# A transform and two MLPs on one core: the buffers' addresses in SBUF moved by 64 and by 192 bytes

## The chip, the cores and the metric

One of the eight cores of one Trainium2 chip runs the program. The metric is the device time of one execution in microseconds (us); three executions were timed, and their median counts.

## The reference

```
X = fft(fft(x, axis=1), axis=2).real          # x: (2, 3008, 256), float32
x = X.reshape(6016, 256)
h = x @ w_in;   x = relu(h)**2 @ w_out         # 256 -> 2048 -> 256
h = x @ w2_in;  x = (h * sigmoid(1.702*h)) @ w2_out   # 256 -> 2048 -> 256
```

## The kernel before

The token axis is split in blocks of 512, 512 and 482 columns for each of the two sequences; features lie on the 128 partitions. A value in float32 is carried as a high part and a low part (type fp32r), and each product is three matmuls: high by high, low by high, high by low.

**Head** (about the first 38 us). The first input `xt` is loaded, folded by VectorE (`fold`, tiles `t` and `xt`) and transformed on TensorE (lines 554, 565, 638, 673). The results become `eo` tiles, the even and odd parts in high and low.

**First MLP.** 96 steps, one for each block of tokens and group of 128 hidden features. A step is six matmuls (`front1`, lines 768 to 770: moving operand `eo`, result `psa`), three VectorE instructions that put `p` and `h` together (lines 1047, 1049, 1050), relu and square on ScalarE (1058, 1059), the high part `gh` on ScalarE (1064), the low part `gl` on GpSimd or VectorE (helper `sub`, line 181), and twelve matmuls (`back`, line 783: moving operands `gh` and `gl`, result `psb`). Six more pairs of matmuls (line 745, `o02N` to `o13N`) take pieces of an `eo` block, that begin at any column, against the constant `sel_t`. Loading and splitting of all weights, and the transform of the later inputs, is interleaved. The order of all of it is written out by hand as a list of names (`ORDER`), run under a manual schedule.

**Second MLP.** 48 units of two hidden groups each. A unit has 21 matmuls (`products`, line 1103: moving operands `ya`, `yb`, `yc`, result `psc`) and 24 matmuls (`back2`, line 1119: moving operands `gh` and `gl`). Between them ScalarE and VectorE form `a1`, `u` and `g` (lines 1150 to 1155, 1186 to 1189), the high part `gh` (1164) and the low part `gl` (181). The order is that of the loop.

**Where the tiles lie.** Each partition of SBUF is filled from two sides. On the left, upward: small constants, the weights (`w`, from address 1408 on; `ya` and `yb` later reuse two of these places), the raw inputs (`raw`), the input tiles, and in the second MLP the pool `m2` with `yc`, `a1`, `u`, `g` and every second `gh`. On the right, downward from the top: a tile `edge` that nothing reads or writes, and under it `mg` (`gh`, `gl`; the pool `m3` takes its place in the second MLP), `m` (`p`, `h`), `ep` (`eo`), `np` (`n`), `zp` (`misc`, `zc`, `zs`) and `cp` (`cst`). Before the change the weights, the right side's large tiles and `m2` begin at addresses that are all the same modulo 512: 1408 for the weights, 151424 for the lowest `eo`, 200576 for a `gh` and 140672 for `yc` each leave 384.

The lines that set the places are these; `edge` and `shift` are read and written by nothing. In the last one (line 768) the weights come from the left side and the moving operand from the right.

```python
small.tile([P, 16], F32, name="shift")
...
edge = tc.alloc_tile_pool(name="edge", bufs=1, side="right")
edge.tile([P, 24], F32, name="edge")
mg = tc.alloc_tile_pool(name="mg", bufs=2, side="right", reuse_waits="tile")
...
T.matmul(o, lhsT=w[:, 0, fs], rhs=t[:, par, 0, 0:wd], start=True, stop=False)
```

Of the kernel before, what the change touches and what calls it, by code (L numbers as in the profile page):

```python
# [9 lines left out]
F32 = mybir.dt.float32  # L10
# [6 lines left out]
P = 128  # L17
# [151 lines left out]
def spectral_two_mlps_kernel(  # L169
# [49 lines left out]
    wq = ctx.enter_context(tc.tile_pool(name="wq", bufs=4))  # L219
    cv = ctx.enter_context(tc.tile_pool(name="cv", bufs=1))  # L220
    edge = tc.alloc_tile_pool(name="edge", bufs=1, side="right")
    edge.tile([P, 24], F32, name="edge")
    mg = tc.alloc_tile_pool(name="mg", bufs=2, side="right", reuse_waits="tile")
    m = tc.alloc_tile_pool(name="m", bufs=2, side="right", reuse_waits="tile")
    ep = tc.alloc_tile_pool(name="ep", bufs=3, side="right", reuse_waits="tile")
# [862 lines left out]

    m2 = tc.alloc_tile_pool(name="m2", bufs=1, side="left", reuse_waits="tile")
    m3 = None  # L1090
    yC[0] = m2.tile([P, 2, 3, NP2], F32R, tag="yc", name="yc")
    units = 8 * BLKS
    run(stage_c(0))
# [256 lines left out]
```

## Time and profile before

| | |
|---|---|
| time, median of 3 executions | 944.34 us (944.24 to 944.53) |
| the profiled execution's own time | 944.28 us |
| its span, first to last instruction | 942.5 us |
| PE busy | 934.3 us, 99% |
| DVE, ACT, POOL busy | 697.9, 566.8 and 267.8 us |
| mean granted TensorE clock | 0.999 of full speed |

The span is what the trace covers; the time is 1.78 us longer than it. The busy time of PE is that of matmuls that overlap, so it says that PE hardly ever sat idle, and not that it ran at its peak. The engines are called PE (TensorE), PEld (its weight loads), DVE (VectorE), ACT (ScalarE), POOL (GpSimd) and SP (SyncE, which issues the DMAs).

### The profile page before, as it was taken

The page shows a single profiled execution, that of the slowest core. Times are in us where ns is not written, and L with a number is a line of the kernel's source. Part 1 is how long each engine was busy: PE and PEld are TensorE (multiplying, and loading weights), DVE is VectorE, ACT ScalarE, POOL GpSimd, SP SyncE. Part 2 cuts the span into 40 slices and gives each one's busy share as a digit, 9 for nine tenths or more (in the row PEclk, how much of TensorE's full clock was granted, in tenths as well). Part 3 has the DMA queues.
Part 4 walks back from the last instruction along what each step waited for, and adds up shares of the span by engine and source line. Part 5 has one row for each costly group of instructions (what it writes and reads, how often), then busy time and mean ns, then how long its engine had stood idle before and what let it go on. Part 6 is the DMA issues. An engine that isn't in the chain of part 4 may idle for free.

```text
span 942.5 us, 10895 instructions
## 1 busy us (share of the span) xinstructions
PE 934.3 (99%) x4272; PEld 778.5 (83%) x4272; DVE 697.9 (74%) x810; ACT 566.8 (60%) x605; POOL 267.8 (28%) x144
## 2 busy tenths in 40 slices
PE   9999999999999999999999999999999999999998
PEld 9688888887877888888888888888888888888886
DVE  7999998988878788887897665665575476476453
ACT  5798997563746767686856544544454455455343
POOL 0665776542453547163123200020020011000000
PEclk9999999999999999999999999999999999999999
DMA  8421434600010041100320100110010011001001
GB/s 312 157 90 45 159 134 140 224 1 1 31 37 1 1 137 43 54 37 0 132 90 1 54 33 1 45 46 1 1 65 22 1 43 46 0 1 45 1 1 42
DMA packets 13058, 53.52 MB, mean 57 GB/s; under 512 B 1360, under 2 KB 4688, under 8 KB 9808
## 3 DMA queue, kind: packets, MB, share of 16 engines
q1 hardware_dynamic: 13008, 52.84, 15.5%
q8 instruction: 33, 0.54, 0.2%
q14 instruction: 17, 0.14, 0.0%
HBM read 37.36 MB, written 15.48 MB: 56 GB/s over the span
## 4 chain that ended last, share of the span: by engine, by line
PE 97%; DVE 2%; DMA 1%; ACT 0%; issue 0%; SPq 0%; DVEq 0%
PE psb L1119 27%; PE psb L783 27%; PE psc L1103 24%; PE psa L768 5%; PE psa L769 5%; PE psa L770 5%; PE psa L638 1%; PE psa L565 1%; PE psa L673 1%; PE psb L638 1%; DMA xt<-in_x 1%; PE psb L565 0%; DVE eo L181 0%; DVE h L1050 0%; DVE t L486 0%; DVE t L490 0%
## 5 line engine op out<-in xcount | busy, mean ns | idle before, releaser
L783 PE MATMUL psb<-gh,w 128*128 128x512 f32 (+1 forms) x768 | 216.0, 387 | 0.0
L181 POOL TENSOR_TENSOR gl<-h,gh 128x1024 fp32r<-128x1024 f32 (+1 forms) x62 | 155.7, 2514 | 136.9 <-PE psb L783 74.6
L783 PEld LDWEIGHTS psb<-gh,w 128*128 128x128 f32 x768 | 144.0, 188 | 28.3 <-issue 0.4
L1119 PE MATMUL psb<-gh,w 128*128 128x512 f32 (+1 forms) x576 | 164.3, 387 | 0.0
L1187 DVE TENSOR_TENSOR g<-u,psc 128x1024 f32<-128x1024 f32 (+1 forms) x48 | 57.6, 1201 | 116.5 <-PE psc L1103 116.5
L1064 ACT CAST gh<-h 128x1024 fp32r<-128x1024 f32 (+1 forms) x96 | 98.4, 1034 | 50.1 <-PE psb L783 34.8
L1189 ACT ACTIVATE g<-g 128x1536 f32<-128x1536 f32 (+1 forms) x48 | 70.4, 1467 | 95.7 <-DVE g L1187 95.7
L1119 PEld LDWEIGHTS psb<-gh,w 128*128 128x128 f32 x576 | 108.3, 188 | 21.1
L783 PE MATMUL psb<-gl,w 128*128 128x512 f32 (+1 forms) x384 | 117.4, 387 | 0.0
L181 DVE TENSOR_TENSOR gl<-g,gh 128x2048 fp32r<-128x2048 f32 (+2 forms) x50 | 110.7, 2217 | 0.4 <-ACT gh L1164 0.4
L1058 ACT ACTIVATE h<-h 128x1024 f32<-128x1024 f32 (+1 forms) x76 | 79.2, 1042 | 23.8 <-DVE h L1050 23.8
L888 POOL TENSOR_TENSOR ue<-raw 128x512 f32<-128x512 f32 (+1 forms) x11 | 19.9, 1832 | 250.9 <-DMA raw<-ydram 244.5
L1164 ACT CAST gh<-g 128x2048 fp32r<-128x2048 f32 (+2 forms) x50 | 90.5, 1814 | 0.1
L1119 PE MATMUL psb<-gl,w 128*128 128x512 f32 (+1 forms) x288 | 88.2, 387 | 0.0
L783 PEld LDWEIGHTS psb<-gl,w 128*128 128x128 f32 x384 | 72.3, 188 | 13.9
L1047 DVE SCALAR_TENSOR_TENSOR p<-n,w1n_t,psa 128x512 f32<-128x512 f32 (+1 forms) x96 | 70.2, 731 | 18.1 <-PE psa L770 17.8
L1059 ACT ACTIVATE h<-h 128x1024 f32<-128x1024 f32 (+1 forms) x76 | 79.7, 1049 | 2.4
L1049 DVE TENSOR_TENSOR h<-p,psa 128x512 f32<-128x512 f32 (+1 forms) x96 | 65.1, 678 | 17.6 <-POOL gl L181 4.3
L768 PE MATMUL psa<-eo,w 128*128 128x512 f32 (+1 forms) x192 | 75.3, 392 | 0.5 <-DVE zc L594 0.3
L769 PE MATMUL psa<-eo,w 128*128 128x512 f32 (+1 forms) x192 | 74.4, 388 | 0.6 <-DVE eo L181 0.6
L1186 ACT ACTIVATE g<-psc 128x512 f32<-128x512 f32 (+1 forms) x48 | 28.4, 592 | 76.6 <-PE psc L1103 76.6
L770 PE MATMUL psa<-eo,w 128*128 128x512 f32 (+1 forms) x192 | 74.4, 387 | 0.0
(178 smaller groups left out, 1530.9 us busy)
## 6 DMA issues: line engine op xcount, KB each, us to landing
ydram<-o SPq DMA_DIRECT2D x14, 512.0 KB, 3.4
xt<-in_x SPq DMA_DIRECT2D x5, 1024.0 KB, 7.1
cst<-in_dfts SPq DMA_DIRECT2D x8, 576.0 KB, 5.7
raw<-in_w1i SPq DMA_DIRECT2D x4, 1024.0 KB, 5.1
raw<-in_w1o SPq DMA_DIRECT2D x4, 1024.0 KB, 6.4
raw<-in_w2o SPq DMA_DIRECT2D x4, 1024.0 KB, 5.7
raw<-in_w2i SPq DMA_DIRECT2D x4, 1024.0 KB, 6.6
raw<-ydram SPq DMA_DIRECT2D x4, 1024.0 KB, 4.8
```

The costliest lines, as they stand in the source:

```text
L181: eng.tensor_tensor(out=o, in0=a, in1=f32(b), op=ALU.subtract)
L768: T.matmul(o, lhsT=w[:, 0, fs], rhs=t[:, par, 0, 0:wd], start=True, stop=False)
L769: T.matmul(o, lhsT=w[:, 0, fs], rhs=t[:, par, 1, 0:wd], start=False, stop=False)
L770: T.matmul(o, lhsT=w[:, 1, fs], rhs=t[:, par, 0, 0:wd], start=False, stop=True)
L783: T.matmul(acc[j][ec][:, s, 0:wd], lhsT=w[:, hl, e0:e0 + P], rhs=(gh, gl)[gi][:, s, 0:wd], start=(first and hl == 0 and gi == 0), stop=(la ...
L1058: A.activation(out=hv, in_=hv, func=AF.Relu)
L1059: A.activation(out=hv, in_=hv, func=AF.Square)
L1064: A.copy(st["gh"][:, :, 0:wd], st["h"][:, :, 0:wd])
L1103: T.matmul(bank, lhsT=w[:, hl, slot * P:(slot + 1) * P], rhs=x[:, yl, 0:wd], start=(first and hl == 0 and yl == 0), stop=(hl == 1), skip_g ...
L1119: T.matmul(o[:, s, 0:wd], lhsT=weights[1, 1, f // 4][:, hl, e0:e0 + P], rhs=g[:, 2 * i + s, 0:wd], start=(f == 0 and hl == 0 and g is gh), ...
L1164: A.copy(gh[:, at], gs[u - 1][:, at])
L1189: A.activation(out=g[:, 1:4], in_=g[:, 1:4], func=AF.Gelu_apprx_sigmoid)
```

## The change

The unused tile `edge` shrinks from 96 to 32 bytes in each partition, so that everything on the right side lies 64 bytes higher. A new unused tile `shift2` of 192 bytes stands ahead of the second MLP's left pool, so that `yc`, `a1`, `u`, `g` and the `gh` in that pool lie 192 bytes higher. The weights, the raw inputs, the input tiles `xt` and `t`, `ya` and `yb` stay where they were.

```diff
     edge = tc.alloc_tile_pool(name="edge", bufs=1, side="right")
-    edge.tile([P, 24], F32, name="edge")
+    edge.tile([P, 8], F32, name="edge")
     mg = tc.alloc_tile_pool(name="mg", bufs=2, side="right", reuse_waits="tile")
...
     m2 = tc.alloc_tile_pool(name="m2", bufs=1, side="left", reuse_waits="tile")
     m3 = None
+    m2.tile([P, 48], F32, name="shift2")
     yC[0] = m2.tile([P, 2, 3, NP2], F32R, tag="yc", name="yc")
```

In the built programs each engine has the same instructions in the same order, with the same waits on the same semaphores at the same counts; line numbers behind the second edit and buffer numbers alone differ. The addresses are:

| tiles | address before (bytes in the partition) | after | modulo 256 before, after |
|---|---|---|---|
| weights `w`, `ya`, `yb`, `raw`, `xt`, `t`, `ue` | 1408 and on | the same | 128, 128 |
| `cst`, `misc`, `n`, `eo`, `p`, `h`, `gh`, `gl`, `o` on the right | 116096 and on | 64 more | 128, 192 |
| `zc` | 132864 | 64 more | 0, 64 |
| `yc`, `a1`, `u`, `g`, `gh` in `m2` | 140672 and on | 192 more | 128, 64 |
| PSUM and DRAM tiles | | the same | |

## Rows read from the trace of the kernel before

**Rows 1.** The page: busy time of each engine; granted clock in 40 slices.

```profile
PE 934.3 (99%) x4272; PEld 778.5 (83%) x4272; DVE 697.9 (74%) x810; ACT 566.8 (60%) x605; POOL 267.8 (28%) x144
PEclk9999999999999999999999999999999999999999
```

**Rows 2.** Windows: stretch, its us, busy us of each engine, granted clock, DMA.

```profile
0.00:38.00 38.00, 35.83 (x241) 30.82 (x242) 32.26 (x55) 21.35 (x48) 10.23 (x13) 1.00 0.77 291
38.00:240.00 202.00, 200.66 (x929) 166.07 (x928) 186.13 (x248) 153.54 (x160) 113.72 (x51) 1.00 0.26 93
240.00:445.00 205.00, 205.00 (x913) 169.19 (x912) 166.31 (x207) 141.12 (x150) 100.05 (x52) 1.00 0.11 39
445.00:607.00 162.00, 162.00 (x716) 134.06 (x715) 119.03 (x119) 93.21 (x95) 22.66 (x16) 1.00 0.13 45
607.00:942.50 335.50, 330.86 (x1481) 278.36 (x1479) 194.13 (x185) 157.53 (x153) 21.09 (x12) 1.00 0.07 25
38.00:138.00 100.00, 99.74 (x440) 81.03 (x439) 94.99 (x127) 90.92 (x93) 68.05 (x28) 1.00 0.29 101
```

**Rows 3.** Waits of PE's matmuls over the span: us, times, longest.

```profile
PE psa L444 <- DVE still L267: 1.1, 1, 1.1
PE psa L638 <- DVE h L1050: 0.8, 1, 0.8
PE psa L769 <- DVE eo L181: 0.6, 1, 0.6
```

**Rows 4.** The chain that ended last, in order of time: start us, us, what.

```profile
32.70 2.52 DVE eo L181
...
35.26 0.50 PE psa L769
...
444.68 2.73 PE psc L1103 x12
...
541.37 2.72 PE psb L1119 x12
...
549.53 2.04 PE psc L1103 x9
...
642.60 2.64 PE psb L1119 x12
```

**Rows 5.** Groups of equal form: count, then busy us, mean ns, idle before.

```profile
L1049 DVE TENSOR_TENSOR h<-p,psa 128x512 f32<-128x512 f32 x64 | 44.0, 688 | 12.9 <-POOL gl L181 3.9 <-DVE p L1047 1.5 <-DMA ydram<-o 1.0
L1153 DVE TENSOR_TENSOR u<-a,psc 128x512 f32<-128x512 f32 x32 | 22.0, 686 | 29.1 <-ACT a L1150 29.1
L1064 ACT CAST gh<-h 128x1024 fp32r<-128x1024 f32 x64 | 66.7, 1050 | 23.3 <-PE psb L783 17.1 <-DVE h L1056 4.3 <-issue 1.1
L368 ACT CAST w<-ue 128x1024 fp32r<-128x1024 f32 x10 | 10.5, 1047 | 0.0
L181 POOL TENSOR_TENSOR gl<-h,gh 128x1024 fp32r<-128x1024 f32 x42 | 108.9, 2597 | 75.5 <-PE psb L783 30.6 <-ACT gh L1064 26.5 <-DVE h L1050 5.8
L181 POOL TENSOR_TENSOR w<-ue,w 128x1024 fp32r<-128x1024 f32 x8 | 23.7, 2958 | 17.0 <-ACT w L368 16.9
```

**Rows 6.** Timeline of TensorE around `o13N` (line 745): start us, us.

```profile
366.92 0.51 PE L745 MATMUL psa<-eo,sel_t 128*128 128x376 f32 x2
367.27 0.40 PE L768 MATMUL psa<-eo,w 128*128 128x512 f32 x1
```

**Rows 7.** Timeline of VectorE and GpSimd at the end of the head.

```profile
29.93 0.94 DVE L181 TENSOR_TENSOR eo<-ht,eo 128x756 fp32r<-128x756 f32 x1
32.61 2.59 DVE L181 TENSOR_TENSOR eo<-ht,eo 128x268 fp32r<-128x268 f32 x1
31.60 3.31 POOL L181 TENSOR_TENSOR w<-ue,w 128x1024 fp32r<-128x1024 f32 x1 [1.77 <-ACT w L368]
```

**Rows 8.** DMA issues by tile (times, KB each, us to landing), and the wait on one.

```profile
ydram<-o SPq DMA_DIRECT2D x14, 512.0 KB, 3.4
DVE h L1049 <- DMA ydram<-o: 1.2, 3, 0.6
```

## The prediction

> **What bounds the kernel now.** I first read the page's busy rows: PE is busy in 99% of the span, DVE in 74%, ACT in 60%, and the granted clock is at its upper level, 2.4 GHz, in all 40 slices [rows 1]. Busy time of overlapping matmuls doesn't show their pace, so next come the windows [rows 2]. From 240 to 607 us PE is busy in every microsecond; from 38 to 240 us it misses 1.3 us, in the first 38 us 2.2, and behind 607 us 4.6, nearly all of it the last copies and the last store. PE's own waits are 1.1, 0.8 and 0.6 us at the longest [rows 3]. So what bounds the kernel is the pace of the matmuls, and no other engine's work, outside a head of some 35 us.
>
> The pace is in the chain by time [rows 4]: twelve matmuls of 512 columns in 2.72 us, 226.7 ns each (nine with `yc` in 2.04, the same), and twelve of 482 columns in 2.64 us, 220.0 each. At 2.4 GHz 512 columns are 213.3 ns and 482 are 200.8, so a matmul of 512 pays 13.3 ns beside its columns and one of 482 pays 19.2. How many there are follows from the code: 96 steps of 18 and 48 units of 45 are 3,888, two thirds of them (2,592) with 512 columns. 2,592 x 226.7 ns + 1,296 x 220.0 ns = 587.6 + 285.1 = 872.7 us of the 942.5. The rest is the head (36 us), the transforms between the steps, the stalls above and the tail.
>
> **The change, part by part.** It adds and removes no instruction. The order on each engine, the waits, their counts, the transfers and their sizes stay. The two edits have one answer, so they are costed together: their cost is the change of each instruction's duration when its operands begin elsewhere. The two tiles themselves cost nothing, since nothing writes them. What the rows say for each engine:
>
> - *DVE and ACT.* The same work on tiles of the right side and of the left takes the same time. A sum of 128x512 takes 688 ns with its tiles on the right and 686 on the left; a cast of 128x1024 takes 1,050 on the right and 1,047 on the left [rows 5]. These tiles begin at the same place modulo 512, so the rows prove only that the side doesn't matter. I take 0 for the change. The ends: below, -2 us (the head's blocked instruction, under the rivals); above, +4.5 us (a rival too). The cover is DVE's idle time, 15.9 us from 38 to 240 us; without it the slower work would show in PE's stalls one for one.
> - *PE.* The moving operands on the right (`eo`, `gh`, `gl`) and in `m2` (`yc`, half of `gh`) move against the weights. Twelve of a unit's products have `ya` and `yb`, which stay: 48 x 12 = 576, and so 3,312 matmuls change their distance from their weights. Before, all these distances are 0 modulo 512, and a trace with one value of the cause can't show its effect. One place differs: line 745, where `eo` is read from column 106 of a block on, 424 bytes into it, against weights that begin at 576. There two matmuls of 376 columns take 0.35 us [rows 6], 175 ns each; 376 columns are 156.7 ns, so each pays 18.3 ns. That is between the 13.3 and the 19.2 of the aligned ones. The nearest row thus says that distance costs nothing, and I take 0. The ends are the only spread in that overhead that the trace shows, 19.2 - 13.3 = 5.9 ns to either side: 3,312 x 5.9 ns = 19.5 us less or more.
> - *POOL.* Its low parts on the right take 2,597 ns in the mean and those of the weights, as large, on the left 2,958 [rows 5]; the 3.31 us of one that lies over a DVE instruction [rows 7] shows what spreads them. I take 0; the ends are those of DVE, since POOL itself idles half of the first MLP.
> - *DMA.* Stores and loads of tiles on the right begin 192 instead of 128 bytes past a multiple of 256. A 512 KB store takes 3.4 us from issue to landing, and in the first MLP waits on it come to 1.2 us in 3 times, of DVE, not of PE [rows 8]. I take 0; even a tenth more on each, 0.34 us, would only lengthen DVE's three waits by 1 us, before the 15.9 us that it has idle.
>
> A rule that speaks against the change is in the Trainium skill, DMA: Bandwidth & Descriptors, section How a descriptor splits into AXI transactions: a piece that doesn't start at a multiple of 256 bytes begins with a transaction from the boundary below, and pays for the bytes ahead. If that holds for the SBUF side, a row of 4,096 bytes goes from 132 beats of 32 bytes to 134, 1.5%, or by an estimate from that page 0.05 us of the store's 3.4; the sum would stay where the rows have it. No run here shows it yet.
>
> The sum: 944.28 us for the profiled execution (942.5 of span and 1.78 around it), plus 0. It lies 0.06 us under the median of 944.34, so the forecast is **944.3 us**. The three times lie within 0.3 us of each other, and 0.2% of the time, 1.9 us, is about what a measurement of this kernel can tell from no change.
>
> **The rivals.**
>
> 1. *PE's reads depend on the distance to the weights, and the new distance is better.* For it: each matmul pays 13.3 or 19.2 ns that its columns don't explain, so there is something to win, and with PE never idle each nanosecond counts 3,312 times, 3.3 us. Against it: rows 6. From 0.57 ns a matmul on it is faster by 1.9 us; at 2.4 ns it gives 8 us, 936.3; at the end, 924.8.
> 2. *The same dependence, and the new distance is worse*: slower, on the other side from no change. For it: the tiles leave the multiples of 128 bytes on which weights and moving operands stood together. Against it: rows 6 again, where the operand begins 40 bytes past a multiple of 256. It decides from 0.57 ns a matmul; at 2.4 ns it gives 952.3, at the end 963.8. In both cases the products with `ya` and `yb` would keep their 226.7 ns.
> 3. *Side engines get slower* because a tile that begins off a 128-byte line costs more per row. From 38 to 138 us DVE is busy for 95.0 of 100 us and PE for 99.7 [rows 2], so this is where it would show. 5.0 us of idle time cover a growth of 5%; PE falls behind by 1.9 us at (5.0 + 1.9) / 95.0 = 7%, about 50 ns on a 690 ns sum. At 10% the loss is 9.5 - 5.0 = 4.5 us: 948.8. Against it: no pair of DVE or ACT in rows 5 differs by more than 3 ns, though none lies off a 128-byte line.
> 4. *The head falls another way.* Ahead of the first hidden step DVE makes `eo` from 128x268 elements in 2.59 us, while 128x756 took 0.94 just before; POOL's 3.31 us instruction lies over the slow one, and PE waits for the result until 35.26 us [rows 4, 7]. A few tens of nanoseconds elsewhere could put DVE ahead of POOL. The gain is at least 2.59 - 0.94 = 1.65 us, 942.6, at most nearly the 2.59: 942.0 is a fair value, just past what can be told.
>
> The Trainium skill, SBUF: State Buffer, section Who interferes with whom, has the rule for the last: VectorE with two SBUF inputs and GpSimd reading SBUF lock each other out for a whole instruction, and nothing else contends. The blocked 2.59 us agree; by that page PE waits for nobody and rivals 1 to 3 would have no cause, but it doesn't speak of addresses, so it doesn't exclude them.
>
> **How the numbers follow.** No change to within 1.9 us: 0.55, which holds the small forms of all four. Rival 1 past 0.57 ns: 0.16. Rival 4, far enough to be told: 0.08. Rival 2: 0.12. Rival 3: 0.09. So faster 0.24, same 0.55, slower 0.21. For the range I go into the PE rivals to 2.4 ns, and no further: 8 us to either side, 936 to 952. That takes in rivals 3 and 4 whole, 0.17, and about half of rivals 1 and 2, 0.14, and with the 0.55 it makes 0.86; since the ends of the unknown are guesses of mine I don't narrow it.
>
> **What would show it.** Right: twelve matmuls of lines 783 and 1119 still take 2.72 and 2.64 us in the chain; the sum at line 1049 stays at 688 ns and the cast at line 1064 at 1,050; PE's busy time in the window from 240 to 607 us is full, and the windows' borders in the program (first product of line 1103 at 444.7 us [rows 4]) haven't moved by more than 1 us. Wrong: a pace other than 226.7 ns on lines 768 to 783 and 1119, and on `yc`, with `ya` and `yb` unchanged (rivals 1, 2); DVE's or ACT's means up by 5% and PE with new waits on `gl` or `psa` before 138 us (rival 3); `eo` of 268 elements under 1 us and the first hidden step ahead of 35 us (rival 4). The prediction is wrong if PE's pace hangs on where its operands lie, which the trace of before couldn't test.

## The result, and the profile after

The changed kernel takes 950.11 us (949.93 to 950.31, 4 executions) against 944.29 us (944.17 to 944.53, 4) of the kernel before on the same chip: a ratio of 1.0061, 95% interval 1.0044 to 1.0079. It is 5.8 us slower. The range of 936 to 952 us holds the time; the forecast of no change was wrong, and it went the way of rival 2.

The page and the windows of the changed kernel, to compare with [rows 1, 2] (stretch, its us, busy us of PE, PEld, DVE, ACT, POOL, granted clock, DMA):

```profile
PE 941.5 (99%) x4272; PEld 779.6 (82%) x4272; DVE 696.4 (73%) x810; ACT 565.9 (60%) x605; POOL 267.1 (28%) x144
38.00:240.00 202.00, 201.79 (x928) 166.16 (x928) 184.56 (x248) 153.28 (x160) 114.87 (x51) 1.00 0.27 93
240.00:445.00 205.00, 205.00 (x907) 168.37 (x906) 166.09 (x206) 139.72 (x149) 100.23 (x52) 1.00 0.11 39
```

PE is busy for 7.2 us more, at the same granted clock and with the same instructions. The other engines are busy for as long as before, or 1.5 us less. From 240 to 445 us PE starts 907 matmuls instead of 913, and isn't idle in either kernel: it is slower, and not kept waiting. Two of its three waits in [rows 3] are as before (us, times, longest), and the one of 0.8 us on `h` is gone:

```profile
PE psa L444 <- DVE still L267: 1.1, 1, 1.1
PE psa L769 <- DVE eo L181: 0.6, 1, 0.6
```

The chain in order of time (start us, us, what) shows the pace. Behind line 1089 the numbers are higher by one.

```profile
446.22 2.74 PE psc L1104 x12
...
546.76 2.75 PE psc L1104 x12
549.51 2.76 PE psb L1120 x12
...
557.13 2.76 PE psc L1104 x12
...
562.66 2.09 PE psc L1104 x9
...
639.11 2.64 PE psc L1104 x12
```

Against [rows 4] twelve matmuls of 512 columns take 2.75 to 2.76 us instead of 2.72, and the nine with `yc` 2.09 instead of 2.04. Twelve of 482 columns take 2.64 us as before (in the first such block of the first MLP 2.67 us, line 783 from 181.14 us on). A unit of 512 columns goes from 541.37 to 551.57 before, 10.20 us, and here from 546.76 to 557.13, 10.37. The first product of the second MLP starts at 446.22 instead of 444.68 us. So 1.5 us are lost up to there, 0.15 of them in the head, and the 32 units of 512 columns, at up to 0.17 us each, lose the rest.

The side engines don't account for it. The groups that answer to [rows 5] (count, then busy us, mean ns) take as long as before to within 0.5%:

```profile
L1049 DVE TENSOR_TENSOR h<-p,psa 128x512 f32<-128x512 f32 x64 | 44.0, 688 | 12.6 <-POOL gl L181 3.9 <-DVE p L1047 1.5 <-ACT ue L294 0.4
L1154 DVE TENSOR_TENSOR u<-a,psc 128x512 f32<-128x512 f32 x32 | 22.0, 687 | 30.3 <-ACT a L1151 30.3
L1064 ACT CAST gh<-h 128x1024 fp32r<-128x1024 f32 x64 | 66.4, 1046 | 24.7 <-PE psb L783 18.5 <-DVE h L1056 4.4 <-issue 1.2
L181 POOL TENSOR_TENSOR gl<-h,gh 128x1024 fp32r<-128x1024 f32 x42 | 109.4, 2609 | 76.5 <-ACT gh L1064 26.5 <-PE psb L783 19.4 <-DVE p L1047 12.0
```

### The profile page after: what moved, and what is told of

Its sections match the earlier page's. It is cut to its first block, busy times and chain, and to the rows that moved or that the text cites. A ratio compares the mean times of both kernels' runs of the same rounds, so it can differ in the third digit from the quotient of the medians.

```text
span 948.3 us, 10895 instructions
## 1 busy us (share of the span) xinstructions
PE 941.5 (99%) x4272; PEld 779.6 (82%) x4272; DVE 696.4 (73%) x810; ACT 565.9 (60%) x605; POOL 267.1 (28%) x144
## 4 chain that ended last, share of the span: by engine, by line
PE 96%; DVE 3%; ACT 0%; issue 0%; DVEq 0%
PE psb L1120 28%; PE psb L783 26%; PE psc L1104 24%; PE psa L768 4%; PE psa L769 4%; PE psa L770 4%; PE psa L638 1%; PE psa L444 1%; PE psa L565 1%; PE psa L673 1%; PE psb L638 1%; DVE h L1050 0%; DVE p L1047 0%; PE psb L565 0%; DVE eo L181 0%; DVE h L1056 0%
```

## The experiments

From start to start of PE's fp32r matmuls, steps over 260 ns left out as stalls, the trace has a mean of 226.9 ns for 512 columns before and 229.8 after, and of 219.9 ns for 482 columns in both. 2.9 ns x 2,592 = 7.5 us; 1.1 us less of PE's idling between 38 and 240 us takes part of it back. The question was what the pace hangs on.

**The two edits apart.** The first run has the first edit alone (`edge` of 8), the second the second edit alone:

```diff
-    edge.tile([P, 24], F32, name="edge")
+    edge.tile([P, 8], F32, name="edge")
```
```diff
     m3 = None
+    m2.tile([P, 48], F32, name="shift2")
```

> The first edit alone: the right side 64 bytes up, the second MLP's left pool where it was. Theory D (a matmul's pace hangs on the distance of its moving operand from its weights, taken modulo some power of two): eo, gl, gh on the right stand 64 bytes off, so the first MLP ends 1.5 us later, at 446.2 us as in the changed kernel; in the second MLP gl and every second gh are off and yc and the other gh are not, so a unit of 512 columns takes about 10.28 us (10.20 before, 10.37 after both edits): some 948 us in all. Theory A (the moving operand's own address off a multiple of 128 bytes costs, wherever the weights are): the same here. Theory S (DVE, ACT, POOL or DMA got slower, and PE waits): PE keeps 2.72 us for twelve matmuls and shows new waits.

> The second edit alone: yc, a1, u, g and every second gh 192 bytes up, the right side where it was. D and A: the first MLP ends at 444.7 us as before; a unit of 512 columns takes about 10.29 us, a unit of 482 columns 9.90 or a little less; some 947 us. If the two edits add up, this run and the one of the first edit lose 5.8 us together. S: some wait of PE's appears in the second MLP alone.

The first took 949.79 us, ratio 1.0057 (1.0042 to 1.0072); the second 947.62 us, 1.0033 (1.0021 to 1.0046); the kernel before took 944.54 us beside them. The chain of the right side alone, and then that of the second MLP's pool alone:

```profile
445.95 2.74 PE psc L1103 x12
...
561.99 2.09 PE psc L1103 x9
564.07 2.75 PE psb L1119 x12
...
572.35 2.04 PE psc L1103 x9
...
577.15 2.72 PE psc L1103 x12
```
```profile
444.62 2.73 PE psc L1104 x12
...
560.67 2.10 PE psc L1104 x9
562.77 2.74 PE psb L1120 x12
565.51 2.72 PE psc L1104 x12
568.23 2.77 PE psb L1120 x12
```

The first MLP is late with the first edit and in time with the second, as all theories of PE's pace had it. Two expectations fell. The edits don't add up: 5.3 and 3.1 us apart, 5.8 together, and the first alone took 949.8 us, not some 948. And in the run of the right side `yc` stood at its old distance from its weights, yet nine of its matmuls took 2.09 us in one unit and 2.04 in the next: a matmul is slowed by neighbours too. The run of the second edit shows how. Behind nine `yc` matmuls that moved by 192 bytes (560.67, 233.3 ns each) come twelve that stand at the old distance (562.77). By their starts in the trace the first five of these take 225 to 236 ns, and from the sixth on each takes 226 or 227. So the place of the matmuls before has an after-effect of some matmuls.

**Absolute places, or distances?** The next run moves both sides up by 64 bytes. The one after it moves the left side alone down by 64, with the second MLP's pool held in place:

```diff
-    small.tile([P, 16], F32, name="shift")
+    small.tile([P, 32], F32, name="shift")
...
-    edge.tile([P, 24], F32, name="edge")
+    edge.tile([P, 8], F32, name="edge")
```
```diff
-    small.tile([P, 16], F32, name="shift")
+    pass
...
+    m2.tile([P, 16], F32, name="shift2")
```

> Everything 64 bytes up: the left side with weights, ya, yb, raw and the second MLP's pool by a larger unused tile, the right side by the first edit. All distances are 0 modulo 512 again, and all moving operands start 64 bytes past a multiple of 128. D: 944.3 us, twelve matmuls in 2.72 and 2.64 us. A: as slow as the changed kernel or slower, 950 us, because now ya and yb are off too.

> The weights and the rest of the left side 64 bytes down, right side and the second MLP's left pool where they were in the kernel before. D: distances of 64 bytes for all moving operands but ya and yb, so the first MLP ends at 446.2 us and a unit of 512 columns takes some 10.3 us: 948 us. A: eo, gh, gl and yc haven't moved, so the first MLP ends at 444.7 us; only ya and yb, 12 of 45 matmuls of a unit, are off: at most 946 us.

Both up: 944.44 us, ratio 0.9999 (0.9990 to 1.0009). Weights down: 950.65 us, 1.0066 (1.0051 to 1.0081). The two chains:

```profile
556.88 2.72 PE psb L1119 x12
559.60 2.04 PE psc L1103 x9
```
```profile
446.21 2.74 PE psc L1104 x12
...
559.80 2.76 PE psb L1120 x12
562.56 2.06 PE psc L1104 x9
```

In the first run the right side lies where it lies in the changed kernel, 64 bytes off a multiple of 128, and nothing is lost as long as the weights lie there as well. In the second nothing on the right has moved, and it is as slow as the change. Theory A falls, and what is left is the distance of the moving operands from the weights. The size of the second was missed: 950.65 us, not some 948. There `ya` and `yb`, whose distance hadn't changed, took 229.4 to 231.8 ns in the mean instead of 226.7 to 227.3, as neighbours of moved ones.

**How far is the period?** The second edit with 128, 256 and 32 bytes instead of 192 (here the first; the others have 64 and 8 for the 32):

```diff
+    m2.tile([P, 32], F32, name="shift2")
```

> The second edit alone with 128 instead of 192 bytes. If distances count modulo 128 or less: 944.5 us and a unit of 512 columns in 10.20 us. If they count modulo 256 or more: a unit over 10.25 us, 946 us or more, as with 192 bytes (947.6).

> The second edit alone with 256 bytes. Modulo 256 or less: 944.5 us. Modulo 512 or more: 946 us or more.

> The second edit alone with 32 bytes. If reads go in pieces of 64 bytes or more, and the first piece begins at a boundary, 32 bytes change little: 944.5 to 945.5 us; if the distance counts byte by byte, 946 us or more.

128 bytes: 948.54 us, ratio 1.0043 (1.0028 to 1.0058). 256 bytes: 944.66 us, 1.0001 (0.9992 to 1.0010). 32 bytes: 948.32 us, 1.0040 (1.0026 to 1.0054). 128 bytes cost and 256 don't, so the distance counts modulo 256; and steps finer than 64 bytes count too.

**The pace by itself.** Behind the kernel's last product groups of matmuls are added, one line of the form below for each; `o` is the moving operand's offset in columns, `ow` that of the weights, `flat` the tile of `yc`:

```diff
+        for k in range(24): T.matmul(pr[:, k % 2, 0:512], lhsT=w[:, 0, k // 2 % 6 * P + ow:k // 2 % 6 * P + ow + P], rhs=flat[:, o:o + 512], start=True, stop=True, skip_group_check=True)
```

> The kernel before with a measurement added at its end, whose results are used by nothing: groups of 24 matmuls each, first of 512 and then of 482 columns, with the moving operand read from yc's tile 0 to 1,024 bytes on and the weights from one weight tile, while the other engines are idle. The added groups lengthen the time by some 230 us. Theory D (the pace hangs on the distance of moving operand and weights, through TensorE's two reads alone): 226.7 ns a matmul at distance 0, about 229 to 230 at 64 bytes, 233 at 192, with both moved by 64 or both by 192 bytes again 226.7; the curve says at which distance it comes back to 226.7, and if moving and weights change places in the difference (weights 64 on) it is slow as well. Theory C (the slower pace comes from the writes of ScalarE, VectorE and GpSimd, which collide with TensorE's reads at some distances): 226.7 at every distance here, since nothing else runs. Theory M (two moving operands that follow each other at different places cost, whatever the weights): a group at one distance has 226.7, the two groups that alternate between two places are slow.

It took 1,185.98 us (one execution). The other engines' busy tenths in 40 slices of its span, then rows of its chain, one group each, its first few matmuls behind the step from the group before included:

```profile
DVE  8999998886878778975575575665655200000000
ACT  6789857465777767654454454544544200000000
POOL 1575755244536440221020020020000000000000
```
```profile
948.65 5.44 PE probe L1219 x24
...
965.35 5.56 PE probe L1222 x24
970.91 5.60 PE probe L1223 x24
...
982.11 5.49 PE probe L1225 x24
...
998.76 5.60 PE probe L1228 x24
...
1009.98 5.60 PE probe L1230 x24
...
1021.17 5.47 PE probe L1232 x24
...
1059.80 5.48 PE probe L1239 x24
1065.28 5.60 PE probe L1240 x24
1070.88 5.48 PE probe L1241 x24
1076.36 5.52 PE probe L1242 x24
...
1087.33 11.12 PE probe L1244 x48
...
1109.49 5.28 PE probe L1246 x24
...
1141.17 5.20 PE probe L1252 x24
```

| line | moving, weights moved by (bytes) | ns a matmul in the steady part |
|---|---|---|
| 1219 | 0, 0 | 226.6 |
| 1222, 1223 | 16 and 32, 0 | 231.6, 233.3 |
| 1225 | 64, 0 | 228.6 |
| 1228, 1230 | 128 and 192, 0 | 233.4, 233.3 |
| 1232 | 256, 0 | 226.7 |
| 1239, 1241 | both 64, both 192 | 227.4, 226.8 |
| 1240, 1242 | 0, 64 and 0, 192 | 233.4, 228.7 |
| 1244 | two at 0 and two at 64 in turn, 0 | 231.7 |
| 1245 | two at 0 and two at 192 in turn, 0 | 230.0 |
| 1246, 1252 | 482 columns: 0 and 160, 0 | 220.0, 216.6 |

The steady part leaves out the first seven starts of a group. Moving the weights by 64 is the same as moving the operand by 192, and the other way round, so it is the difference modulo 256. No other engine works behind 943 us, so theory C falls: PE is slow by itself. Theory M is half right: a group that alternates between 0 and 64 is slower than either alone, while one between 0 and 192 has the mean of the two. With the after-effect in the run of the second edit this fits that the edits didn't add up and that `yc` was slowed where only its neighbours had moved; no run tests that by itself. And 482 columns have a curve of their own, on which 0 is not the best place.

**Whose weights?** A second measurement of the same kind, in which the weights' place alternates:

> The kernel before with another measurement added at its end (about 250 us; its results are used by nothing). First pairs of groups of 48 matmuls in which the weights' place alternates from one matmul to the next, by 64, by 192 and by 128 bytes, and the moving operand follows the place of its own weights in one group, and that of the next matmul's weights in the other. If what counts is the weight load that runs while a matmul's columns stream, which is the next one's, the first group of each pair is slow, at the mean of the two distances of the first measurement (228.7 and 233.3 ns, so 231.0 for 64 and 192 bytes; 233.4 for 128), and the second has 226.7 ns. If a matmul's own weights count, it is the other way round. If only the place in memory counts, both are slow. Then more distances for 512 and for 482 columns; for 482 there were faster ones than at 0 (217.75 ns at 16 bytes, 216.6 at 160, against 220.0), and I look for one under 120 bytes that a tile's spare columns would allow; 512 columns have had none faster than 226.7.

It took 1,206.01 us (one execution). Rows of its chain; lines 1219 and 1220 alternate the weights by 64 bytes, with the operand following its own weights, then the next one's; 1237 and 1243 are 482 columns at 0 and at 24 bytes:

```profile
937.90 10.89 PE probe L1218 x48
948.79 11.11 PE probe L1219 x48
959.90 11.20 PE probe L1220 x48
...
1082.40 5.28 PE probe L1237 x24
...
1114.01 5.13 PE probe L1243 x24
```

11.11 / 48 = 231.5 ns and 11.20 / 48 = 233.3: neither group has 226.7. With 192 bytes it is the same, with 128 the two are at 228.3 and 230.1. If the own weights alone counted, the first of the two at 128 bytes would have 226.7 ns and the second 233.4, and the other way round if the next ones did; both lie between. So this doesn't tell whether the own or the next weights count: what alternating does hides it. For 482 columns, 24 bytes gave 213.4 ns in the steady part, as did 176 and 240; among 23 places it was the only one so fast under 120 bytes.

**A version that uses it.**

```diff
+def cols(wd):
+    return slice(6, 6 + wd) if wd == 482 else slice(0, wd)
...
-            T.matmul(o, lhsT=w[:, 0, fs], rhs=t[:, par, 0, 0:wd], start=True, stop=False)
+            T.matmul(o, lhsT=w[:, 0, fs], rhs=t[:, par, 0, cols(wd)], start=True, stop=False)
...
-                T.matmul(bank, lhsT=w[:, hl, slot * P:(slot + 1) * P], rhs=x[:, yl, 0:wd],
+                T.matmul(bank, lhsT=w[:, hl, slot * P:(slot + 1) * P], rhs=x[:, yl, cols(wd)],
```

The tiles' writers use the same columns.

> A version that uses the measurement: addresses as in the kernel before, but in the blocks of 482 columns every moving operand (eo, gh, gl, ya, yb, yc) begins 6 columns, 24 bytes, into its tile, of whose 512 columns 30 are spare. By theory D and the curve a matmul of 482 columns goes from 220.0 to 213.4 ns and one of 512 stays at 226.7: 1,296 x 6.6 ns = 8.6 us less, 935.9 us; twelve of them in 2.56 us instead of 2.64, a unit of 482 columns in 9.6 us instead of 9.9. If the other engines can't follow a shorter step (their work per step stays), PE shows waits in these blocks and part of it is lost. If the curve holds only while the other engines are idle, 944.4 us.

It took 936.88 us (936.68 to 937.31) against 944.38: 0.9921 (0.9907 to 0.9934), 7.5 us faster than the kernel before and 13.2 faster than the changed one. Its chain:

```profile
543.17 2.72 PE psb L1124 x12
...
604.22 2.77 PE psb L1124 x12
...
631.31 2.56 PE psc L1108 x12
633.87 2.56 PE psb L1124 x12
636.43 1.92 PE psc L1108 x9
```

Twelve of 482 columns take 2.56 us, a unit from 631.31 to 640.91 in the chain, 9.60 us, as expected; the whole is 1.0 us over the expected 935.9. In sum its matmuls of 482 columns take 8.1 us less and those of 512 columns 1.2 us more. Where a block ends, matmuls of both widths stand in one unit, and twelve of 512 columns take 2.77 us there (line 1124 at 604.22), though their own distance is 0. Behind products of 482 columns at 24 bytes eight of the first nine take 228 to 236 ns, and the last three 226 or 227. In the kernel before, where all stand at one place, only the first two behind such a change of width are slow (233 and 231 ns). So the after-effect of another place is the likely cause; it wasn't tested apart.

## Why the prediction was wrong

- **What bounds the kernel** held: PE's pace, with no work of the others between. That is also why a slower pace showed at once, and why little hid it: 1.1 us of idling.
- **The step that failed** is the one on PE: "The nearest row thus says that distance costs nothing, and I take 0." The row was of 376 columns at one distance; the runs showed that 512 and 482 columns each have a curve of their own. For 512 columns a place 64 bytes on costs 2.0 ns and one 192 bytes on 6.7 (lines 1225, 1230), and in the kernel 2.9 ns in the mean, 7.5 us in the place of the 0. 482 columns lost nothing in the mean: those of line 783 went from 220.0 to 220.7 ns, those with `yc` from 219.9 to 217.7. The pair of line 745 takes 0.35 us after the change too (from 368.23 to 368.58 below, to compare with [rows 6]), while 512 columns around it are slower. The prediction said that a trace with one value of the cause can't show its effect, and then let a row of another width decide.

```profile
368.23 0.51 PE L745 MATMUL psa<-eo,sel_t 128*128 128x376 f32 x2
368.58 0.39 PE L768 MATMUL psa<-eo,w 128*128 128x512 f32 x1
```

- **The size** of rival 2 was right in kind, partly by luck: its end of 5.9 ns was the spread between two widths, and the measured cost of the two new distances goes to 6.7 ns. The 3,312 matmuls to which it was applied were the wrong count: those of 512 columns pay, 2,592 of them, `ya` and `yb` among them. That these two would keep their 226.7 ns was wrong; alternating with moved ones they took 228.2 and 230.3 ns in the mean.
- **DVE, ACT, POOL and DMA** came out as priced, at about 0: 688 and 1,046 ns against 688 and 1,050 on DVE and ACT, 2,609 against 2,597 on POOL, and 3.4 us for a 512 KB store in both. Rival 3 fell.
- **The head** (rival 4) fell the same way as before: `eo` of 128x268 took 2.58 us against 2.59 in [rows 7]. The sixteen matmuls of line 638 that follow the head in the chain began 0.15 us later, at 38.21 instead of 38.06 us. With the first edit alone they began at 37.93, so the runs don't put that on the change.
- **The pages.** By the Trainium skill, SBUF — State Buffer, section Who interferes with whom, TensorE reads its moving operand and its weights through two independent ports and waits for no one. The first measurement differs: with every other engine idle, 24 matmuls take 5.44 or 5.60 us by the difference of the two addresses alone. The measurement decides. The rule on DMA transactions that the prediction took from the Trainium skill, DMA: Bandwidth & Descriptors, section How a descriptor splits into AXI transactions, had no visible part in it: a 512 KB store takes 3.4 us before and after, and the prediction's estimate of 0.05 us is too small to show there.
- **Left open:** what in the two reads meets, and whether it is a matmul's own weights or the next one's. That two reads of one engine get in each other's way is the explanation that fits the difference modulo 256; the runs show the difference, not the way.

## What to carry to other kernels

Where PE is busy from end to end, take the pace of its matmuls from the chain of time, and ask why it isn't the columns' own time. Here up to 13 ns of a matmul of 512 columns (226.7 to 240.0) hung on addresses, and no wait shows that. Place the moving operands and the weights of fp32r products at the same address modulo 256 as a start, keep all that alternate at one place, and measure the curve for each width that occurs, since 482 columns were among their fastest at 24 bytes and 512 at 0. A claim that a cause costs nothing needs rows in which the cause differs and all else, the width too, is the same.

## What the runs showed of the hardware

- The pace of fp32r matmuls of 512 columns with a weight load each, from 226.7 ns at a distance of 0 or 256 bytes to 240.0 at 120 bytes, at a granted clock of 1.0 throughout; of 482 columns from 213.3 to 224.4 ns. A shift of 4 bytes is enough: 512 columns take 236.7 ns there (line 1220 of the first measurement).
- Many of the steady paces stand near 213.3, 220.0, 226.7, 233.3 or 240.0 ns, 6.7 ns apart, which is 16 cycles at 2.4 GHz; the runs don't say why.
- Alternating between two distances can be slower than either: 231.7 ns, where they have 226.6 and 228.6 alone. Between 0 and 192 bytes it has their mean, 230.0 ns.
- A place has an after-effect: behind nine matmuls at 192 bytes, five at distance 0 took 225 to 236 ns before the pace was 226.7 again.
